# Attention over memory slots followed by a gated MLP: a new order of the first two blocks and of the loads of v

## Chip, cores, metric

The kernel runs on one core of a Trainium2 chip. The metric is device time in microseconds of one execution; the time before is the median of three runs, 740.7 us (740.14 to 741.76).

## What is computed

Four sequences of 768 tokens with 8 heads of 64 go through chunked attention: each chunk of 32 queries sees 8 memory keys and a window of its own keys, 16 to the left and 8 to the right. Its output, one row of 512 per token, is normalised and passed through a gated MLP of width 1536.

```python
for c in range(nc):                      # 24 chunks of 32
    q_c = q[:, :, c_start:c_end]
    k_full = np.concatenate([mem_k, k_ctx], axis=2)
    v_full = np.concatenate([mem_v, v_ctx], axis=2)
    scores = scale * np.matmul(q_c, k_full.transpose(0, 1, 3, 2))
    a = softmax(scores)                  # with 1e-9 in the denominator
    out[:, :, c_start:c_end] = np.matmul(a, v_full)
xn = x / sqrt(mean(x * x) + 1e-6) * rms_g
out = (silu(xn @ w_gate) * (xn @ w_val)) @ w_out
```

q, k, v are float32; the MLP's weights arrive as 64-bit floats and are turned on the chip into a pair of fp32r tiles, a high part (wh) and a low part (wl); x and the hidden h get the same treatment (xh/xl, hh/hl), and each product takes three matmul passes.

## The kernel before, in words

The 3072 tokens are 8 blocks of 384 tokens. A block's attention is four **units** (two heads each; units 0 to 31 in all), and its MLP runs over 12 slices f of 128 hidden columns: 12 matmuls into pg (gate), 12 into pv (value), 9 into po (output).

The first two blocks (units 0 to 7) are laid out by hand. The string ORDER is read word by word (L816 to L822): a letter is a step, the number is the unit, weight chunk or MLP step, and a last letter d, a or g puts a copy on VectorE (DVE), ScalarE (ACT) or GpSimd (POOL). Every engine, and every DMA queue, does its words in the order of the string. The letters the text uses:

- U: load q and k of a unit on SP's queue (L155 to L157). V: stage v's tile vw (memory values copied in, L185, and the ones column by POOL); w: v's DMAs themselves (dma_v, L188), five or so per unit, on SP's queue or, with a final "a", on ACT's.
- t, T: transposes of q and k on TensorE (PE). Q: copy of q's transpose into qb; n, c, K: copies of k's transpose into kw (left context, right context, own chunk). S: scores s; M, a: row maximum and subtraction; E: exp; P: transpose of the exponentials; C, m: their copies into pt; O: output o; X, x, u: division into x. W: idle matmuls on zeros.
- N, Y: squares of x for the norm; y, z, r: scaling; A, B, D: transpose of x into xh and xl.
- Z: load of the next weight chunk (24 chunks: gate, value, output of each of eight groups; three buffers; chunks 3 to 14 are 1 MB, the others half). J, f, F, I, H, L: the conversion of a chunk: two ACT passes (L508, L509), three DVE passes (L518, L514, L524), the high part (L528, ACT or DVE) and the low part (L532, DVE). Chunk c+3 may be loaded once I of chunk c is done with the buffer.
- g, v, h, i, j, k, l, o: one step of the MLP (gate matmuls, value matmuls, tanh on ACT, two DVE products, hh on ACT, hl on DVE, output matmuls). Steps 0 to 16 (SEQ) cover both blocks as far as f allows; the rest of block 0's slices comes later.

Ahead of the string stand, by hand, the load of the memory keys (mkn), of unit 0's q and k, of the memory values (memV), constants, 26 idle matmuls and four transposes of mkn, whose copy memT POOL needs for kw.

From unit 8 on (line 827 and below) a scheduler places the instructions. The attention of block n+1 is given out in **visits** between the MLP's matmul groups of block n (attn_visits): a visit does S of one unit, O of the unit two before, the transposes of the next unit on DVE (stage_t, L287 and L292, both into tiles named qp and kv), and the loads: load_qk of the unit two ahead (eight DMAs, L165 and L167) and load_v of the next unit (ACT copies the memory values into kv, L185, then five DMAs, L200 to L211). Unit tiles have one buffer there, so v of unit u+1 may be staged only after O of unit u. Block 2's visits (units 8 to 11) stand closer together than the later ones (FIRST, L38).

Of the kernel before, what the change touches and what calls it, by code (L numbers as in the profile page):

```python
# [44 lines left out]


ORDER = """
Z U0 U1 U2 V2a U3 V0a V3d V1g Z J f w1 p1 w3a t0 F I p0 T0 p3 Hd w0 t1 c0d Q0a p2 n0d K0d Q1a L S0
w2 T1 M0 p4 a0 t2 n1a e0 K1a c1d U4 Q2a T2 U5 E0 S1 c2d n2d U6 K2a P0 J p5 M1 Z t3 m0a f C0a S2 a1
Q3a T3 M2 p6 E1 a2 P1 U7 O0 K3a n3d c3d E2 F S3 X0 V4g C1a x0 m1a u0 p7 P2 M3 O1 m2a a3 w4 C2a X1  # L50
V5g E3 O2 x1 u1 P3 X2 V6g x2 m3a w5 t4 u2 C3a I N0 O3 Q4d T4 V7g w6 X3 x3 t5 K4a u3 Ha c4d T5 n4d
Q5a L S4 c5d n5a K5d J Z M4 S5 w7 Y0 a4 f t6 E4 y0 M5 W7 Q6a a5 z0 E5 T6 r0 t7 K6d n6a c6d P4 Q7a
F S6 I C4a T7 M6 m4a Ha a6 A0 K7a c7d A1 n7d B0a L A2 B1a W4 D0 B2a Z D1 A3 J D2 P5 B3a S7 f m5a
W6 D3 M7 C5a O4 F E6 g0 X4 I J Z x4 a7 v0 f h0 F Ha i0 P6 E7 u4 O5 C6a L m6a P7 Z J O6 X5 x5 u5
C7a g1 m7a X6 x6 I O7 j0 Ha u6 X7 N1 x7 L Z u7 v1 k0a F Y1 l0 f o0 h1 J I y1 Ha Z i1 j1 g2 z1 r1
k1a L A13 A11 B13a l1 A10 B11a v2 D13 B10a D11 h2 D10 J i2 A12 o1 j2 B12a J D12 F g3 k2d l2 f o2
h3 I i3 Ha Z v3 F L g4 j3 f k3a l3 v4 I h4 J i4 Z f o3 Ha j4 F g5 k4a L l4 I o4 h5 J Hd Z i5 v5 L
f g6 j5 F k5a I J v6 l5 Ha Z F o5 h6 L i6 j6 g7 F k6a l6 f o6 h7 J I v7 i7 Z Ha f L g8 j7 I k7a v8
l7 Ha f Z h8 o7 J i8 j8 f g9 k8a L l8 v9 F h9 J I o8 i9 Ha Z j9 L g10 k9a F l9 I o9 h10 i10 J Z f
Ha v10 F I g11 j10 Ha F f k10a Z l10 v11 I h11 i11 Ha L g12 j11 J Z L o10 f J F I v12 k11a F Ha  # L60
l11 L h12 Z o11 J i12 L j12 f g13 k12a f l12 I o12 h13 F Z Ha I J i13 v13 f F I g14 j13 J Z L k13a
f Ha l13 v14 Ha L h14 i14 L o13 j14 J Z F I g15 f k14a Ha l14 F L o14 h15 I i15 Ha Z J L v15 f F I
g16 j15 Ha k15a L J l15 v16 f h16 F i16 I o15 j16 Ha L
"""


# [1 line left out]
def tile_kernel(ctx: ExitStack, tc: tile.TileContext, q, k, v, mem_k, mem_v,  # L68
                w_gate, w_val, w_out, rms_g, out):
    nc = tc.nc  # L70
    const = ctx.enter_context(tc.tile_pool(name="const", bufs=1))
    p1 = ctx.enter_context(tc.tile_pool(name="p1", bufs=1))
    p2 = ctx.enter_context(tc.tile_pool(name="p2", bufs=2))
    p3 = ctx.enter_context(tc.tile_pool(name="p3", bufs=3))
# [35 lines left out]
    def psum_a(name):  # L110
        return psa.tile([P, 512], F32, name=name, tag="at")
# [19 lines left out]
    units = [(b, hf, g) for b in range(B) for hf in range(2) for g in range(NG)]  # L131
# [470 lines left out]
    def obuf(name):  # L602
        return p3.tile([P, DM], F32, name=name, tag="stg")
# [39 lines left out]
    manual.__enter__()  # L643
    mkn = obuf("mkn")[0:H * NM].rearrange("p (b e d) -> p b e d", b=B, e=2)
    for e in range(2):
        (nc.sync, nc.scalar)[e].dma_start(out=mkn[:, :, e], in_=mem_k.rearrange("b h m d -> (h m) b d"))
    nc.gpsimd.memset(zero, 0.0)
    nc.vector.memset(memV, 0.0)
    nc.vector.memset(mhalf, -0.5)
# [13 lines left out]
    for a in range(2):  # L663
        o0 = ones[0][:, 0, a:a + 1]
# [5 lines left out]
        o1 = ones[1][:, NJ - 1, a:a + 1]  # L670
# [1 line left out]
                                base=P - RC - 1, channel_multiplier=-1)  # L672
    pm = psum_a("pm")
    pmw.append(pm)
    warm(26)
    for b in range(B):
        nc.tensor.transpose(out=pm[:, b * 64:(b + 1) * 64], in_=mkn[:, b].rearrange("p e d -> p (e d)"),
                            identity=ident[0:64, 0:64])
    for e in range(2):
        r = slice(64 * e, 64 * e + 64)  # L680
        nc.vector.tensor_copy(out=memT[r].rearrange("p g b m -> p b g m"),
                              in_=pm[r, 0:B * 64].rearrange("p (b g e m) -> p b g e m", b=B, g=NG, e=2)[:, :, :, e])
# [4 lines left out]
    def attn_visits(blk, x):  # L687


        us = list(range(blk * NG, (blk + 1) * NG))  # L690
        for n in range(NG + 2):
            with tc.high_priority():
                if 1 <= n <= NG:
                    stage_p(us[n - 1])
                if n < NG:
                    u = us[n]
                    stage_s(u)
                if n >= 2:
# [92 lines left out]
    def tok_o(n):  # L791
# [20 lines left out]
        J=lambda n: w_next(w_open), F=lambda n: w_next(w_clamp), f=lambda n: w_next(w_sign),  # L812
        I=lambda n: w_next(w_shift),
        H=lambda n, *e: w_next(w_high, *e), L=lambda n, *e: w_next(w_low, *e))
    early_open = True
    for tok in ORDER.split():  # L816
# [4 lines left out]
        e = tok[-1] if tok[1:] and tok[-1].isalpha() else ""  # L821
# [106 lines left out]
```

## Time and profile before

| | |
|---|---|
| median of 3 runs | 740.7 us |
| the profiled execution | 741.27 us |
| its span | 739.6 us |
| PE busy | 715.4 us (97%) |
| DVE busy | 383.2 us (52%) |
| ACT busy | 285.0 us (39%) |
| DMA moved | 50.21 MB |
| granted TensorE clock, mean | 0.99 |

The span runs from the first to the last instruction; the execution's own time has some 1.7 us around it. The shares are averages over very different stretches: the first 170 us hold the hand-written string, with the loads and the conversion of all weights, and the rest is MLP with one block's attention between its matmuls. The "..q" engines (SPq, ACTq) are the issue of DMAs by an engine's queue.

### The profile page before, as it was taken

To read this page: it belongs to the slowest core of one execution; us is meant where nothing else is said; L and a number is where in the kernel's file an instruction comes from. 1 tells how busy PE (TensorE), PEld (TensorE's weight loads), DVE (VectorE), ACT (ScalarE), POOL (GpSimd) and SP (SyncE) were. 2 spreads that over 40 slices of the span, in tenths; PEclk is the share of its full clock that TensorE was granted. 3 is DMA by queue.
4 is the path that set the end of the run, shared out by engine and by line. 5 is a ranking of instruction groups with operands and counts; after the bars stand their busy time and mean duration, and the time that the engine had idled before them with its cause. 6 is when DMAs were issued, how large, how long until landed. Compare 5 with 4: busy or idle time off the path is not lost.

```text
span 739.6 us, 13008 instructions
## 1 busy us (share of the span) xinstructions
PE 715.4 (97%) x5114; PEld 655.7 (89%) x5114; DVE 383.2 (52%) x732; ACT 285.0 (39%) x593; POOL 34.5 (5%) x143
## 2 busy tenths in 40 slices
PE   5989989999989999999999999999999999999997
PEld 4878989999878999899998999989998999999996
DVE  4689979886634453454435445344534543342222
ACT  3799646554343232423234222432324222341112
POOL 3300000000000000000000000000000000000000
PEclk7899999999999999999999999999999999999999
DMA  8895344345422132022202222121320220010001
GB/s 184 188 224 170 115 143 142 115 109 119 75 55 66 23 57 46 19 68 49 54 20 63 43 41 50 31 66 23 58 43 20 69 39 19 21 43 1 1 1 43
DMA packets 143175, 50.21 MB, mean 68 GB/s; under 512 B 126985, under 2 KB 134537, under 8 KB 143113
## 3 DMA queue, kind: packets, MB, share of 16 engines
q1 hardware_dynamic: 138726, 44.22, 25.8%
q10 hardware_dynamic: 4386, 5.15, 2.0%
q8 instruction: 40, 0.66, 0.4%
q14 instruction: 23, 0.18, 0.1%
HBM read 43.06 MB, written 6.29 MB: 67 GB/s over the span
## 4 chain that ended last, share of the span: by engine, by line
PE 89%; DMA 4%; DVE 2%; ACT 2%; SPq 2%; issue 1%; ACTq 0%; DVEq 0%
PE pv L561 26%; PE pg L561 26%; PE po L599 26%; PE s L318 3%; PE o L368 3%; PE pT L348 1%; PE xT L440 1%; DMA ws<-in_moe_w_out_dram 1%; DMA kv<-in_v_dram 1%; DMA ws<-in_moe_w_gate_dram 1%; DMA vw<-in_v_dram 1%; SPq L167 1%; SPq L165 0%; ACT pt L227 0%; ACT qb L227 0%
## 5 line engine op out<-in xcount | busy, mean ns | idle before, releaser
L561 PE MATMUL pv<-xh,wh_v 128*128 128x384 f32 x384 | 132.9, 346 | 0.1
L561 PE MATMUL pg<-xh,wh_g 128*128 128x384 f32 x384 | 129.8, 338 | 2.4 <-DVE t L572 2.4
L561 PE MATMUL pv<-xh,wl_v 128*128 128x384 f32 x384 | 129.5, 337 | 0.9 <-DVE wl_v L532 0.9
L561 PE MATMUL pg<-xh,wl_g 128*128 128x384 f32 x384 | 129.5, 337 | 0.0
L561 PE MATMUL pv<-xl,wh_v 128*128 128x384 f32 x384 | 129.3, 337 | 0.0
L561 PE MATMUL pg<-xl,wh_g 128*128 128x384 f32 x384 | 129.3, 337 | 0.0
L572 DVE SCALAR_TENSOR_TENSOR t<-t,pg 128x384 f32<-128x384 f32 x96 | 53.1, 553 | 138.5 <-ACT t L568 138.3
L227 ACT CAST hh<-t 128x384 fp32r<-128x384 f32 x94 | 48.1, 512 | 171.7 <-PE po L599 157.6
L599 PE MATMUL po<-wh_o,hh 128*128 128x512 f32 x285 | 113.9, 400 | 0.3
L599 PE MATMUL po<-wh_o,hl 128*128 128x512 f32 x285 | 113.1, 397 | 0.0
L599 PE MATMUL po<-wl_o,hh 128*128 128x512 f32 x285 | 112.1, 393 | 0.0
L584 DVE TENSOR_TENSOR hl<-t,hh 128x384 fp32r<-128x384 f32 x95 | 52.9, 556 | 99.9 <-ACT hh L227 95.0
L568 ACT ACTIVATE t<-pg 128x384 f32<-128x384 f32 x96 | 47.1, 491 | 143.8 <-PE pg L561 139.0
L575 DVE TENSOR_TENSOR t<-t,pv 128x384 f32<-128x384 f32 x95 | 52.5, 552 | 63.9 <-PE pv L561 63.0
L561 PEld LDWEIGHTS pg<-xh,wh_g 128*128 128x128 f32 x384 | 72.1, 188 | 6.9 <-DVE t L572 3.3
L561 PEld LDWEIGHTS pg<-xl,wh_g 128*128 128x128 f32 x384 | 72.1, 188 | 3.5
L561 PEld LDWEIGHTS pv<-xh,wh_v 128*128 128x128 f32 x384 | 72.1, 188 | 2.7 <-ACT wh_v L227 0.2
L561 PEld LDWEIGHTS pv<-xh,wl_v 128*128 128x128 f32 x384 | 72.2, 188 | 1.2 <-DVE wl_v L532 1.2
L561 PEld LDWEIGHTS pv<-xl,wh_v 128*128 128x128 f32 x384 | 72.2, 188 | 0.4
L561 PEld LDWEIGHTS pg<-xh,wl_g 128*128 128x128 f32 x384 | 72.1, 188 | 0.0
L599 PEld LDWEIGHTS po<-wh_o,hl 128*128 128x128 f32 x285 | 53.5, 188 | 14.0 <-DVE hl L584 1.8
L599 PEld LDWEIGHTS po<-wh_o,hh 128*128 128x128 f32 x285 | 53.5, 188 | 10.0 <-ACT hh L227 1.7
(116 smaller groups left out, 767.0 us busy)
## 6 DMA issues: line engine op xcount, KB each, us to landing
kn<-in_k_dram SPq DMA_DIRECT2D x96, 52.0 KB
qn<-in_q_dram SPq DMA_DIRECT2D x96, 48.0 KB
out_dram<-ob ACTq DMA_DIRECT2D x18, 256.0 KB
ws<-in_moe_w_gate_dram SPq DMA_DIRECT2D x4, 1024.0 KB
ws<-in_moe_w_val_dram SPq DMA_DIRECT2D x4, 1024.0 KB
ws<-in_moe_w_out_dram SPq DMA_DIRECT2D x4, 1024.0 KB
kv<-in_v_dram SPq DMA_DIRECT2D x48, 84.0 KB
kv<-in_v_dram SPq DMA_DIRECT2D x48, 70.0 KB
```

The lines of the kernel that those rows point to most:

```text
L167: nc.sync.dma_start(out=kn[CH * w:CH * w + CH], in_=k[b, h0 + hh, k0:k0 + HT + CH, e:e + CH].rearrange("(c p) d -> p c d", p=CH))
L227: return nc.scalar.copy(out, in_)
L318: on_pe(nc.tensor.matmul(s[64 * par:64 * par + 64, o:o + KC], lhsT=qb[:, c].rearrange("p s q -> p (s q)"), rhs=kw[:, c], start=True, stop= ...
L348: on_pe(nc.tensor.transpose(out=t[:, i * P:(i + 1) * P], in_=pe[:, i * P:(i + 1) * P], identity=ident))
L368: on_pe(nc.tensor.matmul(o[64 * par:64 * par + 64, c0:c0 + D + 1], lhsT=pt[:, i, 2 * par + hh].rearrange("p c q -> p (c q)"), rhs=d["v"][: ...
L440: on_pe(nc.tensor.transpose(out=t[:, i * P:(i + 1) * P], in_=tiles[i][:, kt * P:(kt + 1) * P], identity=ident))
L561: on_pe(nc.tensor.matmul(ps[:, 0:HT], lhsT=weight(a, n, f, kt), rhs=xs[c][:, kt], start=cnt == 0, stop=cnt == 3 * NKT - 1))
L568: nc.scalar.activation(t, g, AF.Tanh, scale=0.5)
L572: nc.vector.scalar_tensor_tensor(out=t, in0=t, scalar=1.0, in1=g, op0=ALU.add, op1=ALU.mult)
L575: nc.vector.tensor_tensor(out=t, in0=t, in1=vv, op=ALU.mult)
L584: nc.vector.tensor_tensor(out=hl, in0=t, in1=hh.bitcast(F32), op=ALU.subtract)
L599: on_pe(nc.tensor.matmul(po[i], lhsT=h[a][:, i * P:(i + 1) * P], rhs=weight(c, "o", f), start=f == 0 and n == 0, stop=f == NF - 1 and n == 2))
```

## The change

- ORDER is a new string: the same steps in another order. In it every v is loaded by SP's queue (the word w3a is gone), the first weight chunk is loaded after q and k of units 0 to 3, all eight c copies and Q4 are on ACT, and there are five W words with 32 idle matmuls in place of three with 17.
- Both halves of mkn are loaded by ACT's queue; SP's queue begins with q and k of unit 0.
- 22 idle matmuls at the start in place of 26, and the transposes of unit 0's q (t0) are put ahead of those of mkn.
- In each visit load_v stands ahead of load_qk.

```diff
-    for e in range(2):
-        (nc.sync, nc.scalar)[e].dma_start(out=mkn[:, :, e], in_=mem_k.rearrange("b h m d -> (h m) b d"))
+        nc.scalar.dma_start(out=mkn[:, :, e], in_=mem_k.rearrange("b h m d -> (h m) b d"))
...
-    warm(26)
+    warm(22)
+    stage_qt(0)
...
+            if n >= 2 and us[n - 2] + 1 < len(units):
+                load_v(us[n - 2] + 1)
             if n < NG and u + 2 < len(units):
                 load_qk(u + 2)
-            if n >= 2 and us[n - 2] + 1 < len(units):
-                load_v(us[n - 2] + 1)
...
 ORDER = """
-Z U0 U1 U2 V2a U3 V0a V3d V1g Z J f w1 p1 w3a t0 F I p0 T0 p3 Hd w0 t1 c0d Q0a p2 n0d K0d Q1a L S0
+U0 U1 U2 V1a U3 V2a V3d V0g Z p1 T0 Q0a p0 t1 n0d c0a p3 w0 K0a Q1a S0 p2 T1 M0 p4 w1 a0 t2 c1a
...
```

On ACT at the start, before: after the two copies of memory values (vw<-memV) come the first weight chunk's passes and the issue of unit 3's v; only then the q copies (qb) that the first scores read.

```order
L227 COPY vw_202<-memV 128x12x64
L227 COPY vw_210<-memV 128x12x64
L508 ACTIVATE ws_192<-ws_192 128x512
L509 ACTIVATE wy_221<-ws_192 128x512
L200 DMA vw_213<-in_v_dram 40x2x64
L211 DMA vw_213<-in_v_dram 56x5x64 x2
L211 DMA vw_213<-in_v_dram 56x6x64 x2
L227 COPY qb_106<-qT_239 64x12x32 x2
L227 COPY qb_107<-qT_273 64x12x32 x2
```

The same place now:

```order
L227 COPY vw_205<-memV 128x12x64
L227 COPY vw_213<-memV 128x12x64
L227 COPY qb_106<-qT_176 64x12x32 x2
L227 COPY kw_239<-kT_228 128x12x8
L227 COPY kw_239<-kT_228 128x13x32
L227 COPY qb_107<-qT_243 64x12x32 x2
L227 COPY kw_224<-kT_283 128x12x8
L227 COPY kw_224<-kT_283 128x13x32
L227 COPY qb_106<-qT_304 64x12x32 x2
L341 ACTIVATE pe_302<-pe_302 128x384
L227 COPY kw_279<-kT_317 128x12x8
L508 ACTIVATE ws_222<-ws_222 128x512
```

The issue of v has left ACT's queue, and the first weight pass has moved behind the copies of units 0 to 2 and the first exp.

On SP's queue in a visit of block 2, before (v of unit 9 stands behind all eight loads of unit 12's q and k):

```order
L165 DMA qn_2216<-in_q_dram 32x12x32 x2
L167 DMA kn_2217<-in_k_dram 32x13x32 x2
L165 DMA qn_2216<-in_q_dram 32x12x32
L167 DMA kn_2217<-in_k_dram 32x13x32
L165 DMA qn_2216<-in_q_dram 32x12x32
L167 DMA kn_2217<-in_k_dram 32x13x32
L200 DMA kv<-in_v_dram 40x2x64
L211 DMA kv<-in_v_dram 56x5x64 x2
L211 DMA kv<-in_v_dram 56x6x64 x2
```

The same visit now:

```order
L165 DMA qn_2234<-in_q_dram 32x12x32 x2
L200 DMA kv<-in_v_dram 40x2x64
L211 DMA kv<-in_v_dram 56x5x64 x2
L211 DMA kv<-in_v_dram 56x6x64 x2
L167 DMA kn_2235<-in_k_dram 32x13x32 x2
L165 DMA qn_2234<-in_q_dram 32x12x32
L167 DMA kn_2235<-in_k_dram 32x13x32
L165 DMA qn_2234<-in_q_dram 32x12x32
L167 DMA kn_2235<-in_k_dram 32x13x32
```

The v loads have moved ahead of six of the eight; two loads of q still stand first.

On ACT around MLP step 6, where weight chunks 9 (wh_g_1315, now wh_g_1306) and 11 (ws_1257, now ws_1267) are converted, before:

```order
L508 ACTIVATE ws_1205<-ws_1205 128x1024
L509 ACTIVATE wy_1253<-ws_1205 128x1024
L227 CAST hh<-t 128x384
L508 ACTIVATE ws_1257<-ws_1257 128x1024
L509 ACTIVATE wy_1293<-ws_1257 128x1024
L227 CAST wh_g_1315<-wy_1201 128x1024
L568 ACTIVATE t<-pg 128x384
```

The same place now:

```order
L508 ACTIVATE ws_1217<-ws_1217 128x1024
L509 ACTIVATE wy_1269<-ws_1217 128x1024
L568 ACTIVATE t<-pg 128x384
L227 CAST wh_g_1306<-wy_1214 128x1024
L227 CAST hh<-t 128x384
L508 ACTIVATE ws_1267<-ws_1267 128x1024
L509 ACTIVATE wy_1343<-ws_1267 128x1024
L568 ACTIVATE t<-pg 128x384
```

The cast of chunk 9 no longer stands behind the passes of chunk 11; the tanh of step 6 (the last row) still does.

## Rows read from the trace of the kernel before

**Rows 1.** The page's first block: busy us, share, instructions of each engine.
```profile
PE 715.4 (97%) x5114; PEld 655.7 (89%) x5114; DVE 383.2 (52%) x732; ACT 285.0 (39%) x593; POOL 34.5 (5%) x143
```
**Rows 2.** Windows, all engines: stretch, length, busy us, PEclk, DMA share, GB/s.
```profile
6.00:17.00 11.00, 3.11 (x30) 2.54 (x30) 4.89 (x11) 3.69 (x7) 3.02 (x14) 0.73 1.02 219
17.00:52.00 35.00, 31.49 (x474) 27.40 (x474) 25.48 (x59) 28.11 (x64) 6.49 (x18) 0.89 0.98 218
...
62.40:101.00 38.60, 37.30 (x198) 34.16 (x198) 33.82 (x49) 25.83 (x44) 0.85 (x1) 1.00 0.45 150
101.00:165.00 64.00, 61.93 (x327) 57.88 (x326) 57.04 (x88) 37.60 (x61) 0.72 (x5) 1.00 0.40 121
165.00:222.00 57.00, 53.29 (x433) 48.38 (x432) 31.36 (x64) 21.70 (x53) 4.06 (x18) 1.00 0.40 81
```
**Rows 3.** Waits of PE, 0 to 222 us: total us, times, longest.
```profile
PE s L318 <- ACT qb L227: 4.7, 1, 4.7
PE qT L237 <- DMA qf<-in_q_dram: 3.2, 1, 3.2
```
**Rows 4.** Timeline of ACT and PE, first scores; then the fifth chunk's cast.
```profile
5.69 1.57 ACT L227 COPY vw<-memV 128x768 f32<-128x768 f32 x2 [1.52 <-DMA memV<-in_mem_v_dram]
...
10.75 4.95 ACTq L211 DMA_DIRECT2D vw<-in_v_dram  x4
...
15.74 1.96 ACT L227 COPY qb<-qT 64x384 f32<-64x384 f32 x4 [4.60 <-DMA vw<-in_v_dram]
...
16.81 1.57 PE L318 MATMUL s<-kw,qb 128*64 128x64 f32 x24 [4.73 <-ACT qb L227]
...
61.37 1.05 ACT L227 CAST wh_v<-wy 128x1024 fp32r<-128x1024 f32 x1
```
**Rows 5.** Windows, ACT alone: stretch, length, busy us, PEclk, DMA share, GB/s.
```profile
24.00:62.42 38.42, 33.81 (x69) 0.99 0.89 209
15.74:62.42 46.68, 38.54 (x79) 0.90 0.85 195
```
**Rows 6.** Groups of ACT by line and shape, 0 to 70 us: busy us, mean ns.
```profile
L227 ACT COPY qb<-qT 64x384 f32<-64x384 f32 x14 | 6.6, 473 | 5.4 <-DMA vw<-in_v_dram 4.6 <-PE qT L240 0.6
...
L398 ACT ACTIVATE junk<-x 128x384 f32<-128x384 f32 x6 | 3.0, 493 | 0.1
L227 ACT COPY kw<-kT 128x416 f32<-128x416 f32 x5 | 2.5, 507 | 0.7 <-DVE kw L230 0.5
L398 ACT ACTIVATION_READ_ACCUMULATOR junk<-x 128x1 f32 x12 | 2.3, 188 | 0.0
...
L508 ACT ACTIVATE ws<-ws 128x512 int32<-128x512 uint32 x3 | 2.0, 660 | 2.7 <-DMA ws<-in_moe_w_gate_dram 2.7
L509 ACT ACTIVATE wy<-ws 128x512 f32<-128x512 f32 x3 | 2.0, 657 | 0.0
...
L227 ACT COPY kw<-kT 128x192 f32<-128x192 f32 x2 | 0.6, 318 | 0.4 <-DVE kw L230 0.3
```
**Rows 7.** Timeline around 100 us: issue of chunk 11, its first pass, the stalled matmul.
```profile
91.41 0.37 SPq L492 DMA_DIRECT2D ws<-in_moe_w_out_dram  x1
...
98.62 1.13 ACT L508 ACTIVATE ws<-ws 128x1024 int32<-128x1024 uint32 x1 [2.34 <-DMA ws<-in_moe_w_out_dram]
...
103.46 0.44 PE L561 MATMUL pg<-xh,wh_g 128*128 128x384 f32 x1 [2.07 <-DVE t L572]
```
**Rows 8.** Timeline of block 2: v staged, v issued, the waiting outputs.
```profile
188.18 0.83 ACT L227 COPY kv<-memV 128x768 f32<-128x768 f32 x1
...
193.24 1.74 SPq L211 DMA_DIRECT2D kv<-in_v_dram  x4
...
196.74 1.17 PE L368 MATMUL o<-kv,qp 128*64 128x65 f32 x24 [1.26 <-DVE qp L287]
...
206.07 0.34 PE L368 MATMUL o<-kv,qp 128*64 128x65 f32 x4 [1.34 <-DMA kv<-in_v_dram]
```
**Rows 9.** Timeline of PE: the fourth unit's scores.
```profile
28.68 0.92 PE L318 MATMUL s<-kw,qb 128*64 128x64 f32 x24
```

More of the change, by code (lines that the diff above doesn't have):

```diff
@@ L47 @@
 ORDER = """
-Z U0 U1 U2 V2a U3 V0a V3d V1g Z J f w1 p1 w3a t0 F I p0 T0 p3 Hd w0 t1 c0d Q0a p2 n0d K0d Q1a L S0
[L49 to L63, printed above, removed]
+U0 U1 U2 V1a U3 V2a V3d V0g Z p1 T0 Q0a p0 t1 n0d c0a p3 w0 K0a Q1a S0 p2 T1 M0 p4 w1 a0 t2 c1a
@@ new lines @@
+K1a n1d e0 T2 Q2a S1 E0 n2d K2d c2a Z J P0 M1 p5 w2 t3 C0a f m0a S2 a1 Q3a T3 p6 M2 E1 U4 a2 P1 w3
+O0 n3d m1a F C1a K3d V4g c3a O1 E2 X0 I U5 S3 x0 V5g J X1 u0 U6 P2 x1 M3 p7 W8 C2a Z f m2a w5 a3
+Ha O2 u1 E3 L V6g P3 X2 t4 F m3a U7 x2 C3a I T4 Q4a w6 u2 O3 K4d c4a N0 n4d V7g X3 S4 x3 w4 u3 t5
+M4 Ha a4 T5 Q5a L T6 c5a n5d Y0 K5d Z K6d t6 w7 n6d c6a y0 E4 S5 Q6a P4 M5 r0 S6 z0 C4a m4a W4 a5
+J M6 t7 E5 f T7 a6 Q7a F P5 n7d K7d m5a A0 c7a I C5a S7 B0a Ha A1 M7 W5 B1a D0 E6 a7 Z A2 J D1 A3
+L O4 B2a f W9 X4 E7 D2 B3a x4 P6 F W6 C6a D3 m6a u4 O5 Z J I O6 X5 f P7 g0 Ha X6 x5 x6 u5 C7a m7a
@@ new lines @@
+u6 v0 h0 F N1 L Z I O7 J X7 i0 Ha x7 g1 j0 u7 k0a L Y1 l0 v1 y1 f Z h1 r1 z1 o0 J i1 F j1 A12 A11
+I B12a A13 B11a g2 D12 k1a Ha l1 Z D11 B13a A10 L v2 B10a h2 D10 J i2 o1 D13 f j2 g3 J F f k2a l2
+v3 I h3 i3 Z Ha o2 f j3 F g4 k3a L l3 I v4 h4 i4 J Z F g5 Ha f j4 I o3 L Ha v5 k4a F Z J l4 L h5
+o4 i5 I g6 j5 Ha f k5a l5 v6 J Z L h6 f o5 i6 F j6 g7 F k6a l6 I J o6 f Z h7 v7 F Ha i7 I g8 j7 Ha
+I k7a l7 Ha v8 Z L h8 i8 J o7 L j8 L g9 k8a l8 F Z J o8 f h9 f v9 F i9 I g10 J j9 Z f k9a Ha F v10
+l9 I h10 i10 o9 Ha I Z j10 Ha L g11 k10a l10 J L o10 h11 F i11 Z J f v11 L f I F g12 Ha j11 I k11a
@@ L64 @@
+Z J l11 v12 f Ha F L h12 i12 o11 L j12 Z J I g13 f k12a F Ha I v13 L Ha l12 L h13 Z J o12 i13 f
+j13 F g14 k13a I l13 Ha L Z J o13 f h14 F I v14 i14 Ha L g15 j14 Z J k14a f l14 F v15 h15 I i15 Ha
+g16 j15 J L f F o14 I Ha L v16 k15a l15 h16 o15 i16 j16
 """
```

## The prediction

> **What bounds the kernel now.** I read the page's shares first, then the windows by stretch, then PE's waits, then the timeline at the places they point to. PE is busy for 715.4 of 739.6 us [rows 1], so 24.2 us of idle time and whatever PE does slowly or for nothing is all that an order can win. The windows show where it is [rows 2]: PE is idle for 7.9 us between 6 and 17 us, 3.5 us between 17 and 52, 1.3 us from 62.4 to 101, 2.1 us from 101 to 165 and 3.7 us from 165 to 222. From 62.4 on PE is the bound, but DVE is busy for 90.9 of the 102.6 us to 165, so there is little room there for weights that come late.
>
> PE's two longest single waits are in the start [rows 3]: 3.2 us for the second unit's q, and 4.7 us for a copy by ACT. The timeline tells why the copy was late: ACT's queue took 4.95 us to issue four loads of v, ACT's next copies began at 15.74, and the first scores only at 16.81 [rows 4]. The reader is to see there that ACT was not computing.
>
> **The change part by part.**
>
> *The start.* q of unit 1 no longer queues behind the weight chunk, and ACT no longer issues v. The memory values now come behind both halves of mkn on ACT's queue. One issue there has no row of its own in the groups; I take 0.7 us later, so the two copies of 1.57 us [rows 4] begin at about 6.4 and end at 8.0 instead of 7.26. The q copy of unit 0 (two of 0.47), the small and the large k copy (0.3 and 0.51) [rows 6] then end near 9.8, and the first scores start near 10 instead of 16.81. The four fewer idle matmuls and t0 ahead of mkn cost nothing: PE has gaps there.
>
> *What of it reaches PE's dense part.* From 17 to 62 us ACT is the fullest engine. The landmark is the cast of the fifth chunk's high part (H of chunk 4), which ends at 62.42 [rows 4]; value matmuls of MLP step 1 wait for it, and from there on both orders do the same kind of work. ACT was busy for 38.54 us between 15.74 and that point [rows 5]. The new order adds ahead of it: the first chunk's two passes (0.66 + 0.66), the squares of unit 4 to 6's x (three of 0.49 and three reads of 0.19, 2.0 in all), eight c copies (no row on ACT has their 96 elements; above nothing, and at most 0.318 each as for 192 elements [rows 6]; I take 0.3, 2.4 in all), Q4 (0.95) and the first cast (512 columns as in the 0.66 us rows; 0.6). It takes away three n copies (0.95) and, net, three K copies (1.5). That is 7.3 − 2.5 = +4.8, so 43.3 us of work, from 8.0 on. To this comes idle time: 4.6 us as from 24 to 62.42 before [rows 5], and some 2.3 us in the first units, where the copies wait for one transpose after another. The cast would end at 8.0 + 43.3 + 6.9 = 58.2, **4.2 us earlier**. With half the idle it is 7.6 us earlier; with all 8.1 us of before and 2 more for q, k or v that come late, 0.9 us. The other limit is the DMA: 98% busy at 218 GB/s between 17 and 52 us [rows 2], and q, k, v of eight units and chunks 0 to 4 (9.6 MB by the shapes) lie ahead of this cast in both orders. At 125 GB/s for the first 6 us and 218 after, they have landed by 47; ACT wants chunk 4 at about 48 for this sum. So it can be kept, and hardly beaten by more than a microsecond; I take **4.0 us**, range 0.9 to 5.5.
>
> The extra idle matmuls (15 more) fill PE's waits in that stretch. If a wait is shorter than its fill, the fill costs at most some 2 us, inside the range.
>
> *Around 100 us.* Chunk 11 is issued at 91.41 and its first pass starts at 98.62; chunk 9's cast stood behind it on ACT, DVE's low part behind the cast, the product behind that, and PE waits 2.07 us [rows 7]. Now the cast stands ahead. DVE has about 9 us of other work between the step that frees chunk 11's buffer and the first pass that reads it, and the load takes 7.2 us, so **2.0 us** go; at worst none, since tanh of step 6 still stands behind chunk 11.
>
> *The visits.* In block 2 v of unit 9 is staged by 189.0 (188.18 + 0.83), but its loads begin at 193.24, behind q and k of unit 12; the output matmuls wait 1.26 us, and 1.34 us for unit 10 [rows 8]. The first wait is put down to DVE, whose product it doesn't read; I take it for the DMA, which landed about then. With v issued from 189.7 on it lands near 194, before PE comes at 195.5. The first matmuls are followed by a second wait of 0.23 us at unit 10, so **2.8 us** go. Unit 11's wait stays (no q or k stood ahead of it). q and k come some 2.2 us later; they were in time by that much, so DVE's transposes may slip by half a microsecond, with no matmul behind them for 8 us. If the wait was DVE's, 1.6 remain: range 1.5 to 3.0. From block 3 on visits lie about 12 us apart, PE has no such waits, and the change is worth nothing.
>
> *Sum.* 4.0 + 2.0 + 2.8 = 8.8, from the profiled execution's 741.27: 732.5. That execution lies 0.6 above the median of the runs, whose scale gives 731.9. I forecast **732.2 us**.
>
> A rule stands against counting ACT's freed queue. The Trainium skill, "DMA: Bandwidth & Descriptors", section "Issuing engines are not separate DMA queues", says that issuing from several engines saves only issue time, which is usually small beside the transfer. This trace disagrees on "small": four issues held ACT for 4.95 us [rows 4]. By the rule the freed queue would be worth next to nothing, the first term would fall to its lower end of 0.9, and the time would be 735.3.
>
> **Rivals.**
>
> *Given back in the weights.* The start wins, but from 62 to 165 us the weights' chain (buffer freed, load, two ACT and three DVE passes) doesn't follow, because DVE has only 11.7 us of slack in 102.6 [rows 2] and the new order spends it elsewhere. For it: that share; against it: DVE reaches the landmark earlier too, and one cast and one copy leave it for ACT. Then the first term is lost and the second or half of it: 741.27 − 2.8 − 1 or so, **737.5**.
>
> *More than that.* The granted clock was 0.73 between 6 and 17 us and 0.89 from 17 to 52 [rows 2]; if PE isn't idle long enough to lose it, the chain through the first units is shorter by up to 3 us more: **729**.
>
> *The clock falls, and it is slower.* Before, after PE's idle stretches the first scores took 1.57 us at the lower of the two levels (1.2 GHz), the fourth unit's 0.92 at 2.4 [rows 4, 9]. The new order has PE ready earlier than ACT, so PE holds some 8 us of idle time up to the landmark; with every microsecond of work at full clock costing 0.7 more at the lower level, the slack is gone after 11 us of such work. Only if about 25 of the roughly 35 us of PE work there ran at the lower level would it lose 10 us beyond the slack and end past 741: **743**. Against it: with 3.5 us of idle in 35 the clock had come back and stayed. The Trainium skill, "TensorE: Matmul & The Clock Gate", section "HAM oscillation", tells of this pattern of short work and waits that brings the clock down again and again.
>
> *The order does not do what it says.* The scheduler still leaves two q loads ahead of v; if more blocks v there, its term falls to 0: 735, within the range.
>
> **Chances.** Forecast (728.5 to 735) 0.60, weights 0.24, more 0.08, clock 0.05, and 0.03 for other losses of the same sign as the clock. The range 728.5 to 739 leaves out the clock, the others and half of "more" and a little of the weights' case. A difference of 0.2% (1.5 us) is about what a measurement of this kernel can tell from none. Slower by more: 0.06; within: 0.05, from the weights' worst end; faster: 0.89.
>
> **What would show it.** First scores near 10 us; the fifth chunk's cast ending near 58; PE with no wait of over 1 us between there and 160; output matmuls of units 9 and 10 without a wait. The forecast is wrong if the cast ends after 61, if PE's idle from 62 to 165 (shifted) grows past 5 us, or if the clock stays low past 25 us.

## The result, and the profile after

| | before | after |
|---|---|---|
| median | 740.42 us (4 runs, 739.48 to 741.76) | 731.76 us (4 runs, 730.66 to 733.20) |
| ratio | | 0.9883, 95% interval 0.9859 to 0.9906 |
| the profiled execution | 741.27 us | 731.54 us |
| its span | 739.6 us | 729.8 us |
| granted TensorE clock, mean | 0.990 | 0.995 |

The changed kernel is 8.7 us faster by the medians and 9.7 us by the two profiled executions. (The profiled execution of before lies 0.9 us above the median of its four runs, that of after 0.2 below.)

The page's first block, which answers to [rows 1]: PE is busy for 715.1 us, nearly as long as before, so nearly the whole gain is PE's idle time.

```profile
PE 715.1 (98%) x5136; PEld 656.6 (90%) x5136; DVE 380.0 (52%) x725; ACT 287.8 (39%) x600; POOL 36.4 (5%) x143
```

Windows of all engines after, with the columns of [rows 2] and each stretch moved back by about as much as the work had moved:

```profile
6.00:17.00 11.00, 8.49 (x97) 7.50 (x99) 3.77 (x9) 6.12 (x14) 3.83 (x17) 0.81 0.96 188
17.00:52.00 35.00, 30.32 (x502) 26.20 (x500) 28.71 (x63) 30.05 (x67) 6.68 (x15) 0.96 1.03 230
...
58.00:96.00 38.00, 37.40 (x203) 34.94 (x203) 34.92 (x48) 28.42 (x42) 1.77 (x1) 1.00 0.49 160
96.00:160.00 64.00, 64.00 (x337) 59.80 (x336) 55.28 (x88) 37.26 (x59) 0.80 (x5) 1.00 0.39 118
160.00:212.00 52.00, 51.07 (x426) 46.71 (x425) 30.24 (x63) 21.37 (x52) 4.02 (x17) 1.00 0.43 88
```

PE's idle time in the five stretches was 7.9, 3.5, 1.3, 2.1 and 3.7 us and is now 2.5, 4.7, 0.6, 0.0 and 0.9. It went from the first units, from step 7 near 100 us and from block 2's visits; between 17 and 52 us there is more of it, although five W words fill some of it.

PE's waits after, 0 to 215 us (engine, what it waited for, total us, times, longest), beside [rows 3]: neither of the two long waits of before is left.

```profile
PE s L318 <- POOL kw L221: 2.5, 1, 2.5
PE pT L348 <- DVE r L386: 1.3, 1, 1.3
...
PE o L368 <- DMA kv<-in_v_dram: 0.8, 1, 0.8
```

How far ahead the new order is, read from the timelines of PE at the same instruction in both traces (start before minus start after):

| instruction | lead, us |
|---|---|
| first scores (16.81, 11.31) | 5.5 |
| output matmuls of step 0 (65.85, 62.96) | 2.9 |
| output matmuls of step 5 (99.14, 95.64) | 3.5 |
| gate matmuls of step 7 (103.46, 97.74) | 5.7 |
| output matmuls of step 17 (179.27, 173.48) | 5.8 |
| gate matmuls of step 22, behind the visits (209.55, 200.18) | 9.4 |
| end of the span (739.6, 729.8) | 9.8 |

So in these two executions the start is worth 2.9 us at step 0 and 3.5 at step 5 (before, a wait of 0.34 us of PE stood between the two), step 7 2.2 us, the visits 3.6 us and everything behind them 0.4 us.

**The start.** Timeline of ACT and PE after, the places of [rows 4]:

```profile
2.23 1.08 ACTq L652 DMA_DIRECT2D memV<-in_mem_v_dram  x2
...
8.11 1.56 ACT L227 COPY vw<-memV 128x768 f32<-128x768 f32 x2 [3.28 <-DMA memV<-in_mem_v_dram]
...
11.31 0.94 PE L318 MATMUL s<-kw,qb 128*64 128x64 f32 x24 [2.45 <-POOL kw L221]
15.87 1.60 PE L318 MATMUL s<-kw,qb 128*64 128x64 f32 x24
...
45.17 1.19 ACT L508 ACTIVATE ws<-ws 128x1024 int32<-128x1024 uint32 x1 [0.39 <-DMA ws<-in_moe_w_gate_dram]
50.28 1.23 ACT L508 ACTIVATE ws<-ws 128x1024 int32<-128x1024 uint32 x1
58.73 1.06 ACT L227 CAST wh_v<-wy 128x1024 fp32r<-128x1024 f32 x1
```

The copies of memory values begin 2.4 us later than before (8.11 for 5.69). Their loads now stand behind both halves of mkn on ACT's queue, but this made their issue only 0.7 us later. Before, on the same timeline:

```profile
1.55 1.09 ACTq L652 DMA_DIRECT2D memV<-in_mem_v_dram  x2
```

So the other 1.7 us lie between the issue and the landing. The first scores are 5.5 us earlier all the same, and no longer wait for ACT but for POOL's memory keys in kw. The two L508 rows are the first passes of chunks 3 and 4; the cast of chunk 4 ends at 59.79 (58.73 + 1.06) where it ended at 62.42.

ACT alone between the end of those copies and that cast (columns of [rows 5]):

```profile
9.67:59.79 50.12, 42.27 (x93) 0.93 0.95 215
```

That is 42.3 us of work and 7.9 us of idle time.

**Step 7.** Timeline after, the places of [rows 7]: chunk 11's issue on SP's queue and its first pass on ACT.

```profile
85.72 0.37 SPq L492 DMA_DIRECT2D ws<-in_moe_w_out_dram  x1
...
93.34 1.16 ACT L508 ACTIVATE ws<-ws 128x1024 int32<-128x1024 uint32 x1
```

The pass waits for nothing, and the gate matmuls of step 7 follow the output matmuls of step 5 after 2.10 us (95.64 to 97.74), which is the pace of the steps around them, where it was 4.32.

**The visits.** Timeline after, the places of [rows 8]: unit 9's v staged and issued, scores of the unit ahead, outputs of units 9, 10 and 11.

```profile
182.39 0.83 ACT L227 COPY kv<-memV 128x768 f32<-128x768 f32 x1
...
184.36 1.74 SPq L211 DMA_DIRECT2D kv<-in_v_dram  x4
...
188.72 0.97 PE L318 MATMUL s<-kv,qp 128*64 128x64 f32 x24
189.47 0.92 PE L368 MATMUL o<-kv,qp 128*64 128x65 f32 x24
...
197.15 0.92 PE L368 MATMUL o<-kv,qp 128*64 128x65 f32 x24
203.22 1.26 PE L368 MATMUL o<-kv,qp 128*64 128x65 f32 x24 [0.80 <-DMA kv<-in_v_dram]
```

Four loads of v start 2.0 us after the staging began, where it was 5.1. Units 9 and 10 have no wait; unit 11's is still there.

### The profile page after: what moved, and what is told of

Its sections match the earlier page's. It is cut to its first block, busy times and chain, and to the rows that moved or that the text cites. A ratio compares the mean times of both kernels' runs of the same rounds, so it can differ in the third digit from the quotient of the medians.

```text
span 729.8 us, 13052 instructions
## 1 busy us (share of the span) xinstructions
PE 715.1 (98%) x5136; PEld 656.6 (90%) x5136; DVE 380.0 (52%) x725; ACT 287.8 (39%) x600; POOL 36.4 (5%) x143
## 4 chain that ended last, share of the span: by engine, by line
PE 92%; ACT 3%; DMA 3%; DVE 1%; issue 0%; POOL 0%; ACTq 0%; SPq 0%; POOLq 0%
PE pv L561 28%; PE po L599 28%; PE pg L561 27%; PE s L318 3%; PE o L368 3%; PE xT L440 1%; PE pT L348 1%; DMA ws<-in_moe_w_val_dram 1%; DMA memV<-in_mem_v_dram 1%; DMA vw<-in_v_dram 1%; ACT junk L398 0%; ACT ws L508 0%; ACT pt L227 0%; DMA kv<-in_v_dram 0%; ACT qb L227 0%
```

## Experiments

Each kernel was timed beside the kernel before on the same chip; a ratio is always to that kernel, with its 95% interval. Variants of the changed kernel are compared with each other by these ratios; the change itself has 0.9883 (0.9859 to 0.9906).

### The visits, alone and undone

`e1_visits_alone` is the kernel before with only this; `e2_visits_undone` is the changed kernel with the two statements in the old order.

```diff
+            if n >= 2 and us[n - 2] + 1 < len(units):
+                load_v(us[n - 2] + 1)
             if n < NG and u + 2 < len(units):
                 load_qk(u + 2)
-            if n >= 2 and us[n - 2] + 1 < len(units):
-                load_v(us[n - 2] + 1)
```

> The kernel before with one part of the change alone: load_v ahead of load_qk in each visit. If both waits of block 2 were for v (theory), the output matmuls of units 9 and 10 come without a wait and the time falls by 2.8 to 3.5 us, to about 737.4. If the wait of unit 9 was for DVE (rival), its 1.26 us stay and the time falls by 1.6. If q and k that come later are missed (second rival), DVE's transposes wait and the gain is under 1 us.

> The changed kernel with load_qk ahead of load_v again. Theory: the parts add up, so the waits of block 2 come back and it is 2.8 to 3.6 us slower than the changed kernel, about 735. Rival: the waits of block 2 came from how the first two blocks end, and with their new order they don't come back: no difference.

Measured: alone 737.21 us (6 runs; 0.9957, 0.9941 to 0.9973), so 3.3 us faster than before's 740.52. Undone 736.30 us (6 runs; 0.9945, 0.9928 to 0.9962), so 4.5 us of the gain are lost; its interval lies wholly above that of the change. PE's waits of the visits alone (165 to 222 us):

```profile
PE o L368 <- DMA kv<-in_v_dram: 1.2, 1, 1.2
```

and with them undone (160 to 222 us):

```profile
PE o L368 <- DMA kv<-in_v_dram: 1.6, 2, 1.4
PE o L368 <- DVE qp L287: 1.1, 1, 1.1
```

The visits alone leave one wait, unit 11's; undone, those of units 9 and 10 are back (unit 10's in two parts, 1.42 and 0.16 us), while unit 11 doesn't wait in that execution. Undone cost more than the 2.8 to 3.6 us that were expected. The wait that the trace puts down to a DVE instruction comes and goes with the place of the loads of v. The DVE did the named transposes at the same distance behind the scores in both kernels (1.48 us before, from 194.51 to 195.99, and 1.47 with the visits alone, from 195.34 to 196.81), and in the second PE didn't wait: the wait was for the DMA, as the prediction took it.

Step 7's stall stays in the visits-alone kernel, so it is another matter. Timeline of PE, then the window from step 5's output matmuls on (PE alone: length, busy us, granted clock, DMA share, GB/s):

```profile
102.73 0.69 PE L561 MATMUL pg<-xh,wh_g 128*128 128x384 f32 x1 [2.13 <-DVE t L572]
...
98.35:110.00 11.65, 9.52 (x40) 0.85 0.36 124
```

In this execution the stall cost more than its wait. The granted clock fell behind it (1.00 before, in the same place), so that ten gate matmuls came every 0.32 us and not every 0.17, and from step 5's output matmuls to step 16's it took 70.91 us where it was 69.29. This may be why the profiled execution, at 738.47 us, is the slowest of the six.

### Unit 3's v by SP's queue, alone

The kernel before, with one word moved.

```diff
-... w1 p1 w3a t0 F I p0 ...
-w2 T1 M0 ...
+... w1 p1 t0 F I p0 ...
+w2 w3 T1 M0 ...
```

> The kernel before with one word of its order changed: v of unit 3 is issued by SP's queue (behind v of unit 2) and not by ACT's. Theory: the 4.6 us wait of ACT's copies goes, the first scores start near 14 instead of 16.81, and one to two microseconds of it reach the end: 739 to 740. Rival by the rule that only issue time is saved: the first scores move, but ACT and the DMA set the pace to 62 us anyway, and the time is the same within 0.3 us.

Measured: 738.74 us (12 runs; 0.9980, 0.9965 to 0.9994), 1.8 us faster. Timeline of PE and ACT: first scores, chunk 3's first pass, chunk 4's cast.

```profile
13.97 1.57 PE L318 MATMUL s<-kw,qb 128*64 128x64 f32 x24 [2.01 <-DVE kw L230]
...
46.53 1.16 ACT L508 ACTIVATE ws<-ws 128x1024 int32<-128x1024 uint32 x1 [1.15 <-DMA ws<-in_moe_w_gate_dram]
...
59.80 1.04 ACT L227 CAST wh_v<-wy 128x1024 fp32r<-128x1024 f32 x1
```

Five issues less on ACT's queue (the row of 4.95 us in [rows 4] holds four of them) bring the first scores forward by 2.8 us and the cast by 1.6. The cast began between 60.59 and 61.37 in the three kernels that have before's order up to there, so 0.8 to 1.6 us of lead is all that single executions show. The Trainium skill, "DMA: Bandwidth & Descriptors", section "Issuing engines are not separate DMA queues", says that issuing from several engines saves issue time alone, which is usually small beside the transfer. Issue time is what was saved here, but it wasn't small, since it lay on the path of ACT's first copies. The gain is smaller than the 4.95 us that the queue was held for: ACT now waits for chunk 3, which SP's queue issues 1.9 us later (41.24 for 39.32), and for chunk 4 by another 1.09 us.

### Chunk 9's cast, undone and alone

`e4_cast_back` is the changed kernel with the cast behind chunk 11's passes; `e12_cast_moved_alone` is the kernel before with only the cast moved.

```diff
-o4 i5 I g6 j5 Ha f k5a l5 v6 J Z L h6 ...
+o4 i5 I g6 j5 f k5a l5 v6 J Z Ha L h6 ...
```

```diff
-f g6 j5 F k5a I J v6 l5 Ha Z F ...
+f g6 j5 F k5a I Ha J v6 l5 Z F ...
```

> The changed kernel with the high-part cast of chunk 9 put back behind the two passes of chunk 11 on ACT. Theory: the stall near 100 us came from this order, so a matmul of step 7 waits again, 1.5 to 2 us, and the time is 1.5 to 2 us longer than the changed kernel's. Rival: the stall is gone because chunk 11 is loaded earlier against PE (issued at 85.72 where step 7 begins at 97.74, before at 91.41 and 103.46 after a stall), and the cast's place costs nothing: no difference.

> The kernel before with one word moved: the high-part cast of chunk 9 ahead of the two passes of chunk 11 on ACT. Theory: the stall of step 7 came from the cast and the low part behind it, so 1 to 2 us of its 2.1 us wait go, and the time falls by 1 to 2 us. Rival: tanh of step 6 still stands behind the late chunk, the product waits for it, and the stall stays: same within 0.3 us.

Measured: undone 733.07 us (6 runs; 0.9907, 0.9888 to 0.9925), 1.3 us above the change, with overlapping intervals. Alone 739.71 us (12 runs; 0.9990, 0.9977 to 1.0002): no difference that can be told from none. Timeline with the cast put back: chunk 11's first pass, then step 7's first gate matmul.

```profile
94.53 1.14 ACT L508 ACTIVATE ws<-ws 128x1024 int32<-128x1024 uint32 x1
...
100.52 0.45 PE L561 MATMUL pg<-xh,wh_g 128*128 128x384 f32 x1 [1.01 <-DVE t L572]
```

Timeline with the cast moved alone: issue of chunk 11, the cast, chunk 11's first pass, step 7.

```profile
91.16 0.37 SPq L492 DMA_DIRECT2D ws<-in_moe_w_out_dram  x1
...
97.37 1.05 ACT L227 CAST wh_g<-wy 128x1024 fp32r<-128x1024 f32 x1 [1.35 <-DVE wy L524]
98.33 1.15 ACT L508 ACTIVATE ws<-ws 128x1024 int32<-128x1024 uint32 x1
...
101.51 0.44 PE L561 MATMUL pg<-xh,wh_g 128*128 128x384 f32 x1 [0.37 <-DVE t L572]
```

In the traces the cast's place does what it should: put back, PE waits 1.01 us even though chunk 11 was there in time; moved alone, the wait falls from 2.07 to 0.37 us although chunk 11's pass begins as long after the issue as before (91.16 to 98.33; it follows the cast directly, so when the chunk had landed can't be read). Yet the median of the kernel with the cast alone hardly moves. One reason can be read: before's profiled execution was 1.3 us above the median of the runs of before beside which this kernel was timed, the other's 0.5 below its own, so 1.8 of the 2.1 us between these two executions is not in the medians. A second is that the stall is not of one size: 2.07 us before, 2.13 with the visits alone (and the clock fell behind it), but 0.30 in the kernel of the section above, where this part of the order is before's as well. There ACT hardly stood for chunk 11 (timeline of ACT and PE):

```profile
95.19 1.18 ACT L508 ACTIVATE ws<-ws 128x1024 int32<-128x1024 uint32 x1 [0.48 <-DMA ws<-in_moe_w_out_dram]
...
100.13 0.45 PE L561 MATMUL pg<-xh,wh_g 128*128 128x384 f32 x1 [0.30 <-DVE t L572]
```

How large the stall is in the executions without a profile is not known; the timed runs allow up to 1.7 us for the cast alone (0.9977) and none.

### Which load comes first, and who issues it

`e5_memv_first` puts the loads of the memory values ahead of mkn on ACT's queue. `e8_mkn_by_both` gives half of mkn back to SP's queue, ahead of unit 0's q.

```diff
-    for e in range(2):
-        nc.scalar.dma_start(out=mkn[:, :, e], in_=mem_k.rearrange("b h m d -> (h m) b d"))
...
+    for e in range(2):
+        nc.scalar.dma_start(out=mkn[:, :, e], in_=mem_k.rearrange("b h m d -> (h m) b d"))
```

```diff
-        nc.scalar.dma_start(out=mkn[:, :, e], in_=mem_k.rearrange("b h m d -> (h m) b d"))
+        (nc.sync, nc.scalar)[e].dma_start(out=mkn[:, :, e], in_=mem_k.rearrange("b h m d -> (h m) b d"))
```

> The changed kernel with the memory values' loads ahead of the memory keys' on ACT's queue. The changed kernel's first copies waited for the memory values until 8.1 us and its first scores began at 11.31, not near 10. Theory: the values land 1.5 to 2.5 us earlier, POOL's and ACT's first copies with them, the first scores begin near 9.5, and about half of it reaches the fifth chunk's cast: 0.5 to 1 us faster than the changed kernel. Rival: the keys come later by as much, kw is late instead, and the first scores don't move; or the DMA sets the pace up to the fifth chunk, and the time doesn't change.

> The changed kernel with the first half of the memory keys on SP's queue again, ahead of unit 0's q and k, as before the change. Theory: q and k of units 0 to 3 come 0.8 us later but the memory values 0.7 us earlier, and the values were what the first copies waited for: first scores within 0.7 us of the changed kernel's, time the same within 0.5 us; this part of the change is worth nothing. Rival: unit 0's q sets the start, and it is 0.5 to 1 us slower.

Measured: memory values first 732.78 us (5 runs; 0.9898, 0.9873 to 0.9922), mkn by both queues 731.96 us (5 runs; 0.9886, 0.9861 to 0.9910). Neither differs from the change. With the values first, ACT's copies begin at 6.14 us but the first scores only at 13.39, since the keys are late (PE's transposes of them begin at 9.91, in the change at 6.91), as the first rival had it. With mkn by both, the first scores are the earliest of all; timeline of PE and ACT (first scores, first passes of chunks 3 and 4, cast):

```profile
9.67 0.94 PE L318 MATMUL s<-kw,qb 128*64 128x64 f32 x24 [1.15 <-POOL kw L221]
...
44.18 1.11 ACT L508 ACTIVATE ws<-ws 128x1024 int32<-128x1024 uint32 x1 [2.12 <-DMA ws<-in_moe_w_gate_dram]
50.03 1.15 ACT L508 ACTIVATE ws<-ws 128x1024 int32<-128x1024 uint32 x1 [0.91 <-DMA ws<-in_moe_w_val_dram]
...
58.88 1.03 ACT L227 CAST wh_v<-wy 128x1024 fp32r<-128x1024 f32 x1
```

The reader is to see that a lead of 1.6 us at the first scores (0.7 at most had been expected) ends as 3.0 us of waiting for two chunks, and the cast starts at 58.88 where the change has 58.73.

### Idle matmuls: one more, or none

`e6_fill_ahead_of_scores` adds a W word ahead of the first scores; `e7_no_fill` takes all five away.

```diff
-... K0a Q1a S0 p2 ...
+... K0a Q1a W14 S0 p2 ...
```

```diff
-... p7 W8 C2a ...   ... m4a W4 a5 ...   ... M7 W5 B1a ...   ... f W9 X4 ...   ... F W6 C6a ...
+... p7 C2a ...      ... m4a a5 ...      ... M7 B1a ...      ... f X4 ...      ... F C6a ...
```

> The changed kernel with 14 idle matmuls (about 2 us) in PE's wait ahead of the first scores. In the changed kernel's trace the clock fell at 13 us, after that wait of 2.45 us, and the second unit's scores took 1.60 us; in another run of the same order with a wait of 2.06 us it stayed and they took 0.97. Theory: with the fill the clock stays at the upper level, the second scores take 0.95, and the fifth chunk's cast ends 0.5 to 1.5 us earlier: 730.3 to 731.3. Rival: PE isn't on the path there, ACT and the DMA are, and the time is the same within 0.3 us.

> The changed kernel without the 32 idle matmuls of its order (five places, some 4.7 us of PE time). Theory: they stand in waits of PE and cost nothing, and the waits are too short for the clock to fall: same within 0.5 us. Rival one: the clock falls without them, the transposes and scores of units 4 to 7 take 1.7 times as long, 1 to 3 us slower. Rival two: they were longer than the waits, 0.5 to 2 us faster.

Measured: one more 733.60 us (6 runs; 0.9904, 0.9877 to 0.9931), none 732.68 us (6 runs; 0.9897, 0.9871 to 0.9922); both agree with the change. With one more, the window of all engines from 6 to 17 us, and ACT's first pass of chunk 3:

```profile
6.00:17.00 11.00, 9.79 (x141) 8.64 (x141) 4.58 (x11) 7.12 (x16) 4.21 (x19) 1.00 0.96 191
```

```profile
46.52 1.10 ACT L508 ACTIVATE ws<-ws 128x1024 int32<-128x1024 uint32 x1 [3.25 <-DMA ws<-in_moe_w_gate_dram]
```

The granted clock stayed at 1.00 (2.4 GHz) where it was 0.81 in the change, and the second scores took 0.97 us in place of 1.60; ACT then waited 3.25 us for chunk 3, and the cast began at 61.03. Without any fill the clock was 0.91 between 17 and 40 us, the cast began at 59.57, and the time is the same. Over all timed runs the mean granted clock was 0.990 to 0.995 without fill and 0.995 to 1.000 with one more, and the medians don't follow it. So in the new order the clock in the first units is not what sets the end.

### Chunk 3 earlier and later

`e9_chunks_earlier` asks for chunk 3 right behind unit 4's v (and for chunk 4 where the change asks for chunk 3); `e10_chunks_earlier_mkn_both` is that together with mkn by both queues; `e11_chunk3_later` asks for chunk 3 behind unit 7's v.

```diff
-... m3a U7 x2 ... X3 S4 x3 w4 u3 t5
+... m3a U7 w4 Z x2 ... X3 S4 x3 u3 t5
...
-... D0 E6 a7 Z A2 ...
+... D0 E6 a7 A2 ...
```

```diff
-... K5d Z K6d t6 w7 n6d ...
+... K5d K6d t6 w7 Z n6d ...
```

> The changed kernel with weight chunk 3 loaded ahead of v of units 6 and 7, and chunk 4 ahead of v of unit 7 (v of unit 4 moved ahead of that of unit 6). Theory: since the change the loads set the pace from 17 to 60 us, and ACT's passes of chunks 3 and 4 wait for them or stand close behind; chunk 3 lands 2 us earlier and chunk 4 1 us, and the fifth chunk's cast ends up to 1 us earlier where ACT was waiting: 0.3 to 1 us faster than the changed kernel. Rival: ACT's own work sets the pace there, and the time is the same within 0.3 us; or v of unit 6 or 7 is late, and output matmuls wait: up to 1 us slower.

> The same, and the first half of the memory keys on SP's queue as before the change. With the keys there the first scores began at 9.67 and not at 11.31, and ACT then waited 2.12 us for chunk 3 and 0.91 for chunk 4: the lead of the start was lost to the loads. Theory: with the chunks earlier those waits shrink, more of the lead gets through, and the fifth chunk's cast ends near 57.5 instead of 59.9: 1 to 2 us faster than the changed kernel, 730 to 731. Rival: the bytes ahead are the same, only their order changed, and some other load is late in their place: same within 0.5 us.

> The changed kernel with weight chunk 3 loaded behind v of unit 7 and not ahead of it. Theory: the loads set the pace, chunk 3 lands 1.3 us later, ACT waits for it, and the fifth chunk's cast ends 0.5 to 1.3 us later: 0.5 to 1.3 us slower. Rival: ACT sets the pace and comes to chunk 3 later than it lands anyway: no difference.

Measured: later 735.74 us (12 runs; 0.9940, 0.9922 to 0.9958), 4.0 us above the change and wholly above its interval. Timeline of SP, ACT and PE with chunk 3 later: its issue, its first pass, the transposes behind it, chunk 4's cast.

```profile
42.46 0.39 SPq L496 DMA_DIRECT2D ws<-in_moe_w_gate_dram  x1
...
48.43 1.10 ACT L508 ACTIVATE ws<-ws 128x1024 int32<-128x1024 uint32 x1 [3.85 <-DMA ws<-in_moe_w_gate_dram]
...
51.86 0.87 PE L348 MATMUL pT<-ident,pe 128*128 128x128 f32 x3 [4.64 <-DVE r L386]
...
63.66 1.03 ACT L227 CAST wh_v<-wy 128x1024 fp32r<-128x1024 f32 x1
```

An issue that is 2.9 us later (42.46 for 39.59) makes ACT wait 3.85 us, with an exp behind the pass, and so PE 4.64; the cast is 4.9 us later. That is more than was expected, for two reasons. The pass begins 3.3 us later than in the change (48.43 for 45.17), not 1.3. And behind PE's wait the granted clock fell, to the lower level (1.2 GHz) for 4 us (window of PE alone):

```profile
51.80:56.00 4.20, 4.14 (x54) 0.50 0.22 52
```

At that level 47 output matmuls took 2.85 us, where 48 of them took 1.74 in the change, and ACT stood for PE: between this pass and the cast it did the same 21 instructions (12.7 us, 12.9 in the change) with 2.5 us of idle time and not 0.7.

Earlier: 731.84 us (6 runs; 0.9886, 0.9867 to 0.9905); with mkn by both 732.06 us (6 runs; 0.9885, 0.9858 to 0.9912). The same as the change, although the trace of the first shows what was hoped for (timeline of SP and ACT: issue of chunk 3, its pass, the cast):

```profile
36.16 0.39 SPq L496 DMA_DIRECT2D ws<-in_moe_w_gate_dram  x1
...
43.12 1.17 ACT L508 ACTIVATE ws<-ws 128x1024 int32<-128x1024 uint32 x1
...
56.67 1.03 ACT L227 CAST wh_v<-wy 128x1024 fp32r<-128x1024 f32 x1
```

Its cast begins 2.1 us earlier than in the change, without a wait for the chunk. But this execution took 729.40 us, the lowest of its six, and their median is not below the change's.

Put side by side, the traces tell how to read this. For the change and the seven kernels that differ from it only in the start, all times in us:

| kernel | first scores | chunk 4's cast begins | span | from there to the end |
|---|---|---|---|---|
| the change | 11.31 | 58.73 | 729.8 | 671.1 |
| memory values first | 13.39 | 59.97 | 730.9 | 670.9 |
| mkn by both queues | 9.67 | 58.88 | 729.9 | 671.0 |
| one more W word | 11.09 | 61.03 | 731.9 | 670.9 |
| no W word | 11.40 | 59.57 | 730.5 | 670.9 |
| chunks earlier | 11.02 | 56.67 | 727.6 | 670.9 |
| chunks earlier, mkn by both | 9.89 | 58.17 | 728.9 | 670.7 |
| chunk 3 later | 11.35 | 63.66 | 734.7 | 671.0 |

The last column is the same within 0.4 us while the cast moves by 7.0: what reaches the cast reaches the end, microsecond for microsecond, and the first scores tell little about either. By the same measure the visits undone have 675.2 behind the cast (4.1 more than the change) and chunk 9's cast put back 672.2 (1.2 more), close to the 4.5 and 1.3 us of the timed runs. But one execution's cast is a sample. These last two kernels have the change's order up to the cast, and theirs began at 58.10 and 60.37, 2.3 us apart. Chunk 3 later stands clear of them by more than that (3.3 us above the higher one), the chunks earlier don't (1.4 below the lower one): the early cast may belong to the one execution that was profiled. The other five were not seen. No version was found that beats the change.

## Why the prediction was right, step by step

The time (731.76 for 732.2) and the sign came out as forecast; the terms of the sum less exactly, read from the two traces: start 3.5 for 4.0, step 7 2.2 for 2.0, visits 3.6 for 2.8, together 9.3, and 0.4 us behind them for which there was no term. At the place for which the first term was worked out, the end of chunk 4's cast, the lead is 2.6 us (62.42 to 59.79); the other 0.9 come between there and step 5, without a term. That the sum came so near is therefore in part luck: the start was overestimated by 1.4 us there, and what lies behind it underestimated by 2.4.

- **The start: the mechanism was right, its beginning was off.** The step "0.7 us later" for the copies of memory values was mis-sized: it is right for the issue of their loads (2.23 for 1.55), but they are 2.4 us later (8.11 for 5.69 [rows 4]) and end at 9.67 where the prediction had 8.0. POOL, for which the prediction had no term, copies memory values too and only then its memory keys into kw, so the first scores start at 11.31 and not near 10. The length of the rest of ACT's walk came out, 50.1 us for 50.2, though by two errors that cancel: 42.3 us of work and 7.9 of idle time against 43.3 and 6.9. So the cast ended at 59.8 in place of 58.2. (ACT was not "the fullest engine" there: by [rows 2] PE was busier, 31.49 of 35 us against 28.11. That the cast hangs on ACT's row of work holds all the same.) The c copies, for which no row stood, took 0.24 us each; 0.3 had been taken.
- **The DMA as the other limit: right that it can hardly be beaten, wrong in where it bites.** The prediction let the loads land by 47 us and named chunk 4. It is chunk 3: it is issued at 39.59, no earlier than before (39.32), and ACT stands 0.39 us for it. So ACT's work and this load end together in the change. In other executions of the same order ACT stood for chunk 4 as well (1.14 and 1.03 us with chunk 9's cast put back). The rate of 218 GB/s was a mean over two stretches, as the section on the hardware shows. That the load binds is shown from both sides: with ACT or PE earlier, the lead turns into waiting for chunk 3 (2.12 and 3.25 us) and no time is won that could be measured; with the load 2.9 us later, 4.0 us are lost, part of it by the clock.
- **ACT's freed queue.** It is worth something by itself: 1.8 us (ratio 0.9980, 0.9965 to 0.9994, so 0.4 to 2.6 us) for one of the change's parts, where the rule that the prediction set against it would have given next to nothing.
- **Step 7.** Its wait is gone in the trace, for both reasons named: the cast's place (put back, 1.01 us of wait return) and a chunk 11 that ACT no longer stands for, since it is issued 9.9 us ahead of step 5's output matmuls (85.72 to 95.64) and not 7.7. In timed runs the cast's place is worth 1.3 us undone and 0.2 alone, both within the uncertainty; in the traces, counted from chunk 4's cast to the end, 1.2 and 1.8 (676.4 us for 678.2 before). This term rested on one execution's load of 7.2 us, and is the least sure of the three.
- **The visits.** The two waits are gone and unit 11's stayed, as said; the price was short by 0.8 us. A group that waits costs more than the idle time that the profile shows: see below.
- **The rivals.** "Given back in the weights" fell: PE is idle for 0.6 us between 58 and 160 us. "More than that" didn't come, since the loads cap the start. "The clock falls" came in part: the second scores took 1.60 us at the lower level, but the clock was back for most of the stretch from 17 to 52 us (0.96), and a run that kept it up won nothing. The Trainium skill, "TensorE: Matmul & The Clock Gate", section "HAM oscillation", tells of work and waits that bring the clock down again and again; in the change that is seen for a few microseconds alone. The order did what it says: two loads of q ahead of v are no hindrance.

What stays open: first, how the 3 to 5 us that the medians leave for the start (8.7 less 3.3 to 4.5 for the visits and 0.2 to 1.3 for the cast) divide among its parts. Taking away mkn's new queue or the idle matmuls changes nothing that can be measured. The order of the first units' words was not undone by itself. Nor do the traces confirm the size: the cast began between 60.59 and 61.37 us in three kernels with before's order and between 58.10 and 60.37 in three with the new one, so single executions allow 0.2 to 3.3 us at the cast. And whether the lower clock of the start (0.83 before between 17 and 40 us, 0.94 after) cost the kernel before anything was not tested in it.

## What to carry to other kernels

In a start that is bound by loads, look up when each load is issued and when its first reader comes, and order the queue by that: one weight chunk two or three words later cost 4 us, while first scores anywhere between 9.7 and 13.4 us changed nothing. Where a short wait recurs behind a queue, put the load that is read next ahead of those that are read in two rounds; this was the surest part of the gain, and the cheapest. A wait seen in one profile can be a matter of that execution: undo the part and time it before counting it. And find an instruction behind which all variants take equally long, as behind chunk 4's cast here: up to there a trace can be compared with a trace, and its spread from one execution to the next is seen.

## What the runs showed of the hardware

- **The rate of the loads goes with which loads they are.** Windows of all engines after, two parts of the stretch from 17 to 52 us:

```profile
17.00:40.00 23.00, 20.36 (x340) 17.96 (x338) 18.31 (x43) 19.27 (x48) 6.68 (x15) 0.94 1.04 192
40.00:52.00 12.00, 9.95 (x165) 8.24 (x163) 10.41 (x21) 10.79 (x20) 0.00 (x0) 1.00 1.00 302
```

  The DMA engines are full in both (1.04 and 1.00), but move 192 GB/s while it is mostly q, k and v, and 302 once the 1 MB chunks flow; before, 182 and 288. A landing time worked out with the mean of both is too early for what stands in the first part.

- **A wait costs more than its idle time.** Before, unit 9's wait was 1.26 us [rows 8], but the step from the output matmuls of one MLP step to the next took 10.15 us and takes 8.42 without it: 1.73. The rest is in two places. A group that doesn't wait starts before the one ahead has ended (scores to outputs 0.75 us, where the scores' row lasts 0.97), which the wait takes away; and the 24 matmuls behind the wait took 1.17 us, not 0.92. Unit 10's step likewise fell by 1.85 us (9.53 to 7.68) where 1.57 were shown.

- **The clock's fall is not the same in each run.** Four kernels whose order is the change's up to there (visits undone, cast put back, chunk 3 earlier, chunk 3 later) show waits of 2.06, 2.85, 1.91 and 2.70 us ahead of the first scores and second scores of 0.97 us, at 2.4 GHz; the change itself and the kernel without W words, which also has its order up to there, show waits of 2.45 and 2.43 us and second scores of 1.60, at 1.2 GHz. So the length of the wait alone doesn't tell.

- **A wait can cost the clock behind it.** Behind PE's wait of 4.64 us (chunk 3 later) the granted clock was 0.50 for 4 us, and behind one of 2.13 us near 100 us (visits alone) ten matmuls came at half the pace, 1.6 us more, while the kernel before, after 2.07 us in the same place, kept 1.00. Of 51 timed runs of the kernel before, the 18 with a mean granted clock of 0.990 or less have a median of 741.4 us, the other 33 739.7. Which of the two, the longer wait or the lower clock, makes those runs longer can't be told from them.

- **A load of 1 MB doesn't always take as long.** Chunk 11 is read 5.35 us after its issue in one kernel (unit 3's v by SP's queue) and 7.21 and 7.26 in two others (before, visits alone), at the same place of the order and with ACT standing for it in all three.
